# A conditioned block with a long convolution and a gated MLP on one core: block 0 in four real products, two split pieces at the start of stages 1 and 2, and another order of the turns

## The chip, the cores and the metric

The kernel runs on one core of a Trainium2 chip. The metric is the device time of one execution in microseconds (us), the median of several runs. All inputs are bfloat16 and come from HBM.

## The reference

There are 2048 rows x of 576 columns. From a condition vector c comes a modulation of six rows of 576, by one small matrix product. The first half of the block is a layer norm with shift and scale, multiplied by a long causal convolution of a gated sequence; the second half is a layer norm with shift and scale and a SwiGLU MLP with 4608 hidden columns.

```python
mod = (silu(c) @ w_mod).reshape(1, 6, 1, -1)         # sa, ca, ga, sb, cb, gb
h  = layernorm(x) * (1 + ca) + sa
kv = conv4(k, shift_k) * v                           # 4 taps along the rows, per column
y  = causal_conv(kv, ssm_k) + kv * ssm_D             # 2048 taps per column
x  = x + ga * (h * y)
h  = layernorm(x) * (1 + cb) + sb
x  = x + gb * ((silu(h @ w1) * (h @ w3)) @ w2)
```

## The kernel before

**Blocks of the convolution.** The rows are cut into eight blocks of 256. A block's kv rows and a block's filter taps are each taken through a short transform, which is a matrix product on TensorE with cosine and sine matrices (`Fb` for rows, `Fk` for taps). A block has 128 frequencies for even and 128 for odd indices. The spectrum X of kv has six planes of 576 columns: real part, imaginary part and their sum, twice (`x_spectrum`, with the sums added by `x_sums`). The filter's spectrum W has four planes (`w_spectrum`); from the W of two neighbouring blocks DVE makes V, again with six planes (`v_block`). A complex product is so done with three real products, X times V plane by plane (`pair`), and the results of all pairs of blocks that belong to one output block are added in z. `real_parts` and `inverse` bring z back to rows: two matrix products for the even and two for the odd frequencies for each half of the rows. Then ScalarE copies the result out, DVE multiplies it with the gate and adds it to x (`residual`), the second layer norm is taken (`quick_stats` on DVE or `ln_sums` on ScalarE), and the normed rows go to `h2row`.

**Turning rows.** The MLP needs its input with the columns on the partitions. `turn_all` turns 256 rows from `h2row` to `h2T`, for the first two blocks on TensorE and later by two transposing loads on SyncE's queue (L819). `modulate` then applies shift and scale to five tiles, on ScalarE (L834) or, with quick, on DVE (L832). `h2row` is one buffer, `h2T` two.

**The MLP.** It runs over four stages of 512 rows, so one stage takes two blocks, an even and an odd one. A stage has a stream and a down projection. The stream goes over nine pieces of four chunks of 128 hidden columns. For each piece w1 and w3 are loaded into one of three buffers (`load_w13`, L965 and L966); TensorE does the gate and the up product (L1014 and L1025), ScalarE the silu and a copy, and DVE their product (L1039). The buffer `wst[2]` also holds the four slots of w2 in the down projection, where two halves of 288 columns are done one after the other, each in nine w2 pieces (L1123, L1134). A w2 piece is loaded into a slot when the piece four before it is done.

**Order.** Block 0 is written out by hand in `first_block`, with the order of TensorE, ScalarE and DVE fixed. It ends with block 0's turned rows. Then `conv_second` (block 1's convolution) runs beside `stream` on block 0's 256 rows alone, for `N1 = 24` of the 36 chunks. Stage 0 does the odd 256 rows of those chunks (short pieces of 256 rows, whose weights are loaded again, but for the last two) and all 512 rows of the other twelve. Beside each stage r = 0, 1, 2 runs `conv(2r + 2)`, the convolution of the next stage's two blocks. It is a generator whose steps have a cost in us, mostly DVE time; after each piece of MLP work `advance` gives it time at a rate `CONV_US[r] / time`. `end` runs what is left of it.

In stage r's down projection the next stage's odd block ends:

```python
if h == 1 and f0 // W2C == TURN and r + 1 < NRB:
    self.end()
    self.turn_all(2 * r + 3)
    if 2 * r + 5 < NBLK:
        self.pair_taps(2 * r + 5)
    self.modulate(2 * r + 3, r > 0)
```

The even block of the next stage is turned and modulated earlier, within `outcome` of the odd one. Older X and V come back from DRAM on SyncE's queue (`get`), some of them during the down projections. Within an engine the build puts instructions in an order by their dependencies and by estimated times, so that later work can stand ahead of earlier work where nothing forbids it; `behind` and `issue_after` forbid it.

**Taps.** The taps of a block are loaded either as they lie (`load_k`) and turned on TensorE (`k_rows`), which is so for blocks 0 and 1, or by a transposing load (`load_taps`, L303), after which `pair_taps` sorts the rows into pairs with four copies from SBUF to SBUF (L312) into `kT`, a single buffer.

Of the kernel before, what the change touches and what calls it, by code (L numbers as in the profile page):

```python
# [25 lines left out]
FC = 4  # L26
# [3 lines left out]
CONV_US = (72.0, 97.0, 108.0)  # L30
RATE1 = 1.8
FIRST_DUE = 12.0
N1 = 24
# [5 lines left out]
TURN = 7  # L39
# [9 lines left out]
class _Kernel:  # L49
    def __init__(self, ctx, tc, q, k, v, shift_k, ssm_k, ssm_D, w1, w3, w2, c, w_mod, out):  # L50
# [21 lines left out]
        self.last_w2 = None  # L72
# [66 lines left out]
    def early_loads(self):  # L139
# [10 lines left out]
        self.load_mod(0, 3)  # L150
# [154 lines left out]
    def pair_taps(self, s):  # L305

        nc = self.nc
        self.kT = self.kvp.tile([P, 2, D], BF16, name="kT", tag="kT")
        taps = self.knat[:].rearrange("p a b -> p (a b)")
        for half in range(2):  # L310
            for cc in range(2):
                nc.sync.dma_start(self.kT[64 * half:64 * half + 64, cc, :],  # L312
                                  taps[cc:P:2, half * D:(half + 1) * D])
# [347 lines left out]
    def first_block(self):  # L661
# [17 lines left out]
        self.waves(0)  # L679
        self.warm(3, self.h2T[0][:, 0, :])  # L680
        sums = [self.small.tile([P, 1], F32, name="l1" + k, tag="sr" + k) for k in "um"]
        self.run_all(self.k_rows(0))
        self.cond_silu()
        self.warm(4, self.h2T[0][:, 0, :])
# [6 lines left out]
        self.load_k(1)  # L691
        self.run_all(self.w_spectrum(0))
        self.cond()
        self.run_all(rows)
        mean, rstd = self.quick_stats(x1[:, 1, :], "l1")
        nmr = self.small.tile([P, 1], F32, name="l1nm", tag="nmr1")
        nc.gpsimd.tensor_mul(nmr[:], mean, rstd)
        nc.gpsimd.tensor_single_scalar(nmr[:], nmr[:], -1.0, op=ALU.mult)
        self.run_all(self.x_spectrum(0))
        self.run_all(self.v_block(0))  # L700
# [4 lines left out]
        self.load_gb()  # L705
        self.whole_turns(0, True)
        self.waves(0, True)
        X, V = self.X[0], self.V[0]
        self.accs[0] = z = self.acc.tile([P, 6, D], BF16, name="z0", tag="z0")
        for o in (0, 3):  # L710
            nc.vector.tensor_add(X[:, o, :], X[:, o + 1, :], X[:, o + 2, :])
            nc.vector.tensor_mul(z[:, o:o + 3, :], X[:, o:o + 3, :], V[:, o:o + 3, :])
            nc.vector.tensor_add(z[:, o + 1, :], z[:, o, :], z[:, o + 1, :])
            nc.vector.tensor_sub(z[:, o, :], z[:, o, :], z[:, o + 2, :])
        self.mod_piece(2)
        self.ln_sums(x1, 0, sums[0], sums[1], 0)
        scales = [self.ln_shift(*self.ln_var(*sums, "l1", nc.gpsimd), nc.gpsimd), (rstd, nmr)]
# [559 lines left out]
```

## Time and profile before

The median of three runs is 509.51 us (508.95 to 510.03). The profiled execution spans 507.3 us, with a mean granted TensorE clock of 0.997.

| stretch, us from the start | what runs | length | PE busy | DVE busy |
|---|---|---|---|---|
| 0 to 33.7 | block 0 | 33.7 | 29.14 | 27.87 |
| 33.7 to 66 | MLP for block 0's rows, block 1's convolution | 32.3 | 32.22 | 29.33 |
| 66 to 123.5 | stage 0, stream | 57.5 | 55.00 | 52.80 |
| 123.5 to 164.7 | stage 0, down | 41.2 | 38.33 | 36.82 |
| 164.7 to 242.2 | stage 1, stream | 77.5 | 77.50 | 60.71 |
| 242.2 to 281 | stage 1, down | 38.8 | 37.74 | 20.53 |
| 281 to 358.9 | stage 2, stream | 77.9 | 77.78 | 73.71 |
| 358.9 to 396.7 | stage 2, down | 37.8 | 37.01 | 18.43 |
| 396.7 to 467 | stage 3, stream | 70.3 | 70.30 | 13.31 |
| 467 to 507.3 | stage 3, down and the end | 40.3 | 35.52 | 5.82 |

PE is TensorE, PEld its weight loads (which run beside the matmuls), DVE is VectorE, ACT ScalarE, POOL GpSimd, SP SyncE, and SPq the queue on which SyncE issues transfers. A line of the order of time has the start, the time, the engine, the line of the kernel, the operation, the tiles (written from read), the number of instructions, and in brackets how long the engine was idle before it and what ended that. Stage boundaries are taken from TensorE's first matmul of each.

### The profile page before, as it was taken

Reading aid. Unit: us, or ns where it says so; the run is one execution under the profiler, and the core shown is the slowest. Engines: PE = TensorE matmul, PEld = TensorE weight load, DVE = VectorE, ACT = ScalarE, POOL = GpSimd, SP = SyncE. Lnnn points to the kernel's source line nnn. Section 1 sums busy time; section 2 is a strip of 40 time slices with the busy share of each in tenths; the row PEclk is TensorE's granted clock in tenths of the full one; section 3 lists DMA queues with packets and bytes.
Section 4 is the critical chain, followed back from the end, with each engine's and each line's share of the span. In section 5 each row is a group of like instructions: output and inputs, shape, how many; then the busy total and the mean of one; then the engine's idle time right before and its main releaser. Section 6 shows DMA issues by size and latency. Waiting matters only on the chain.

```text
span 507.3 us, 8873 instructions
## 1 busy us (share of the span) xinstructions
PE 490.5 (97%) x3530; PEld 287.9 (57%) x3530; DVE 339.3 (67%) x448; ACT 283.9 (56%) x565; POOL 23.2 (5%) x43
## 2 busy tenths in 40 slices
PE   6999999999998999999999999999999999999996
PEld 2767775547776444343777443434677544444774
DVE  8799899898997586997176999799762321112012
ACT  5758679659343588569450455976824355555000
POOL 4200000000001000000000000000000000000000
PEclk9989999999999999999999999999999999999999
DMA  8987997759999895358799996644575554460562
GB/s 281 329 190 217 293 296 205 203 172 311 269 365 299 281 327 166 111 148 250 202 294 332 309 301 226 209 116 165 154 176 125 170 177 140 143 187 1 140 170 65
DMA packets 115037, 107.99 MB, mean 213 GB/s; under 512 B 20339, under 2 KB 107572, under 8 KB 114996
## 3 DMA queue, kind: packets, MB, share of 16 engines
q1 hardware_dynamic: 114974, 107.41, 71.3%
q8 instruction: 28, 0.46, 0.4%
q14 instruction: 13, 0.11, 0.1%
q10 hardware_dynamic: 22, 0.01, 0.0%
HBM read 92.46 MB, written 9.44 MB: 201 GB/s over the span
## 4 chain that ended last, share of the span: by engine, by line
PE 68%; DVE 12%; DMA 9%; ACT 4%; issue 2%; SPq 1%; POOL 1%; POOLq 0%; DVEq 0%; ACTq 0%
PE ps L1014 29%; PE ps L1078 14%; PE ps L1134 14%; PE ps L1025 4%; DMA V<-Vd 4%; DVE p L438 3%; DMA wst<-in_B_w_dram 2%; PE ps L333 2%; DMA kh<-in_A_k_dram 2%; PE ps L572 2%; PE ps L347 1%; ACT junk L469 1%; DVE og L1159 1%; DVE z L440 1%; DVE z L433 1%
## 5 line engine op out<-in xcount | busy, mean ns | idle before, releaser
L1014 PE MATMUL ps<-h2T,wst 128*128 128x512 bf16 (+1 forms) x1056 | 200.8, 341 | 0.9 <-ACT h2T L834 0.3
L1134 PE MATMUL ps<-wst,h 128*128 128x288 bf16 x1152 | 145.5, 286 | 4.6 <-DMA wst<-in_B_w_dram 3.3
L1014 PEld LDWEIGHTS <-wst 128*128 128x128 bf16 x1056 | 100.2, 98 | 86.8 <-issue 15.3
L1134 PEld LDWEIGHTS <-h 128*128 128x128 bf16 x1152 | 112.5, 98 | 36.3 <-issue 7.2
L1032 ACT ACTIVATE h<-ps 128x512 bf16<-128x512 f32 x108 | 64.8, 600 | 79.8 <-PE ps L1025 51.6
L1078 PE MATMUL ps<-h2T,wst 64*128 64x512 bf16 x648 | 70.3, 376 | 0.0
L1036 ACT CAST u<-ps 128x512 bf16<-128x512 f32 x108 | 63.3, 586 | 0.0
L438 DVE TENSOR_TENSOR p<-X,V 128x3456 bf16<-128x3456 bf16 x28 | 54.7, 1954 | 4.6 <-DMA V<-Vd 4.0
L440 DVE TENSOR_TENSOR z<-z,p 128x3456 bf16<-128x3456 bf16 x28 | 54.6, 1951 | 0.1
L1078 PEld LDWEIGHTS <-wst 64*128 64x128 bf16 x648 | 31.3, 94 | 38.3 <-DVE og L1159 0.2
L1105 DVE TENSOR_TENSOR h<-h,u 128x1024 bf16<-128x1024 bf16 x18 | 12.5, 692 | 58.1 <-ACT u L1102 58.1
L1039 DVE TENSOR_TENSOR h<-h,u 128x1024 bf16<-128x1024 bf16 x54 | 36.9, 685 | 14.1 <-ACT u L1036 14.1
L1099 ACT ACTIVATE h<-ps 128x512 bf16<-128x512 f32 x36 | 21.5, 597 | 39.8 <-PE ps L1078 39.8
L469 ACT ACTIVATE junk<-x 128x576 bf16<-128x576 bf16 x54 | 37.1, 687 | 3.1 <-DVE x L587 2.5
L1159 DVE TENSOR_TENSOR og<-ps,gbrow 128x576 bf16<-128x576 f32 (+1 forms) x18 | 12.3, 687 | 36.8 <-PE ps L1134 36.3
L1025 PE MATMUL ps<-h2T,wst 64*128 64x512 bf16 (+1 forms) x264 | 33.3, 341 | 0.1
L1102 ACT CAST u<-ps 128x512 bf16<-128x512 f32 x36 | 20.9, 580 | 0.0
L1025 PEld LDWEIGHTS <-wst 64*128 64x128 bf16 x264 | 8.5, 94 | 21.5 <-issue 18.9
L834 ACT ACTIVATE h2T<-h2T,sbcol,cbcol 128x256 bf16<-128x256 bf16 x20 | 10.4, 590 | 18.2 <-DMA h2T<-h2row 18.2
L599 ACT ACTIVATE h2row<-x,l2n,l2r 128x576 bf16<-128x576 bf16 (+1 forms) x24 | 13.8, 654 | 9.2 <-DVE l2n L487 9.2
L367 DVE TENSOR_TENSOR kv<-kv,p 128x1152 bf16<-128x1152 bf16 x24 | 18.1, 753 | 0.3
L361 DVE TENSOR_TENSOR p<-kh,shk 128x3456 bf16<-128x3456 bf16 x8 | 15.6, 1953 | 0.6 <-ACT shk L210 0.6
(142 smaller groups left out, 366.2 us busy)
## 6 DMA issues: line engine op xcount, KB each, us to landing
wst<-in_B_w_dram SPq DMA_DIRECT2D x80, 512.0 KB, 5.0
wst<-in_B_w_dram SPq DMA_DIRECT2D x72, 288.0 KB, 3.9
wst<-in_B_w_dram SPq DMA_DIRECT2D x80, 64.0 KB, 3.2
kh<-in_A_k_dram SPq DMA_DIRECT2D x7, 720.0 KB, 6.6
X<-Xd SPq DMA_DIRECT2D x5, 864.0 KB, 5.9
V<-Vd SPq DMA_DIRECT2D x5, 864.0 KB, 6.0
Xd<-X SPq DMA_DIRECT2D x4, 864.0 KB, 7.9
Vd<-V SPq DMA_DIRECT2D x4, 864.0 KB, 5.2
```

What stands on the lines that cost most here:

```text
L438: nc.vector.tensor_mul(p[:], X[:], V[:])
L440: nc.vector.tensor_add(z[:], z[:], p[:])
L469: self.nc.scalar.activation(junk[:], src[:, i, :], func, scale=scale, accum_out=out[:, col:col + 1])
L1014: nc.tensor.matmul(gus[k][:, i, a * n:(a + 1) * n], w[:, 5 * i + ct, (fi + a) * P:(fi + a + 1) * P], hT[:, ct, t0:t1], start=(first and ct ...
L1025: nc.tensor.matmul(gus[k][:, i, a * n:(a + 1) * n], w[rows, 4, (fi + a) * P:(fi + a + 1) * P], hT[rows, 4, t0:t1], start=(first and a == 0 ...
L1032: nc.scalar.activation(self.h3[:, f:f + m, t0:t1], gus[k][:, 0, :].rearrange("p (a t) -> p a t", a=m), ACT.Silu)
L1036: nc.scalar.copy(self.u[:, k % 2, :], gus[k][:, 1, :])
L1039: nc.vector.tensor_mul(h3, h3, self.u[:].rearrange("p b (a t) -> p (b a) t", a=m))
L1078: nc.tensor.matmul(gus[k][:, i, :], ws[fc][rows, 5 * i + ct if ct < 4 else 4, cols], hT[rows, ct, :], start=swap == 0 and ct == 4, stop=sw ...
L1099: nc.scalar.activation(h3, gus[k][:, 0, :], ACT.Silu)
L1102: nc.scalar.copy(self.u[:, k % 2, :], gus.pop(k)[:, 1, :])
L1134: nc.tensor.matmul(acc[t], self.h3[:, f0 + f, t * P:(t + 1) * P], w[:, f, :], start=(f0 + f == 0), stop=(f0 + f == NF - 1))
```

## The change

It has four parts. Block 0 no longer makes V and its three-product form; it multiplies X with W in four real products a parity, and TensorE adds them in the inverse product, which so has eight terms instead of four for each half of the rows, one of them with a negated cosine matrix (`minus`). What block 1 needs of V, X's sums and its own filter spectrum goes to `conv_second`; block 1's taps come by a transposing load. Statistics of both halves of block 0's rows are taken early on DVE, mod piece 2 is done ahead of `x_spectrum`, and w_mod's first three pieces come in three loads. Second, `N1` is 28: seven pieces, not six, run beside block 1. Third, in stages 1 and 2 the first two pieces run for the even 256 rows and then for the odd ones, so that the odd rows may come later: the convolution beside the stage before goes on into the stream, and the next one begins after the even pieces. Fourth, the turns of the even blocks wait (`pending`) for a set place in the down projection, and `pair_taps` uses two copies instead of four and stands at the last w2 piece. For the last stage the odd rows are still turned within the down projection, at piece 8 instead of 7.

```diff
-CONV_US = (72.0, 97.0, 108.0)
+CONV_US = (72.0, 104.0, 118.0)
-N1 = 24
+N1 = 28
-TURN = 7
+EVEN, MOD, TURN = 4, 6, 8
+SOLO = 2
+QUICK1 = True
@@ early_loads
-        self.load_mod(0, 3)
+        for m in (2, 1, 0):
+            self.load_mod(m, 1)
@@ pair_taps
-            for cc in range(2):
-                nc.sync.dma_start(self.kT[64 * half:64 * half + 64, cc, :],
-                                  taps[cc:P:2, half * D:(half + 1) * D])
+            nc.sync.dma_start(self.kT[64 * half:64 * half + 64], taps[:, half * D:(half + 1) * D])
@@ first_block
+        minus = self.kvp.tile([P, P], BF16, name="minus", tag="Wo")
+        nc.gpsimd.tensor_single_scalar(minus[:], self.Fb[:, 0, 0], -1.0, op=ALU.mult)
+        self.cond_silu()
         self.warm(3, self.h2T[0][:, 0, :])
         self.run_all(self.k_rows(0))
-        self.cond_silu()
-        self.warm(4, self.h2T[0][:, 0, :])
+        self.cond()
+        self.warm(3, self.h2T[0][:, 0, :])
...
-        self.load_k(1)
+        self.load_taps(1)
         self.run_all(self.w_spectrum(0))
-        self.cond()
         self.run_all(rows)
-        mean, rstd = self.quick_stats(x1[:, 1, :], "l1")
...
-        self.run_all(self.x_spectrum(0))
-        self.run_all(self.v_block(0))
...
+        self.pair_taps(1)
+        scales = [self.quick_stats(x1[:, cc, :], "l1") for cc in range(2)]
+        self.mod_piece(2)
+        self.run_all(self.x_spectrum(0))
         self.whole_turns(0, True)
+        z = [self.acc.tile([P, 6, D], BF16, name=f"z{i}", tag=f"z{i}") for i in range(2)]
+        for e in range(2):
+            Xe = X[:, 3 * e + 1:3 * e + 3, :]
+            nc.vector.tensor_mul(z[e][:, 0:2, :], Xe, W[:, 2 * e:2 * e + 2, :])
+            nc.vector.tensor_mul(z[e][:, 2:4, :], Xe, _ap(W, (2 * e + 1) * D, [[-D, 2], [1, D]]))
...
+            nc.scalar.activation(hg[:, cc, :], x1[:, cc, :], ACT.Identity, bias=nmr[cc][:, 0:1], scale=scales[cc][1])
         self.waves(0, True)
-        for o in (0, 3):
-            nc.vector.tensor_add(X[:, o, :], X[:, o + 1, :], X[:, o + 2, :])
-            nc.vector.tensor_mul(z[:, o:o + 3, :], X[:, o:o + 3, :], V[:, o:o + 3, :])
-            nc.vector.tensor_add(z[:, o + 1, :], z[:, o, :], z[:, o + 1, :])
-            nc.vector.tensor_sub(z[:, o, :], z[:, o, :], z[:, o + 2, :])
...
-        ps = [self.inverse(0, cc) for cc in range(2)]
+        ps = [whole(cc) for cc in range(2)]
         self.run_all(self.gate(0))
-        self.run_all(self.k_rows(1))
         self.mod_columns()
-        self.run_all(self.w_spectrum(1))
@@ outcome
+                self.turn_pending()
                 for cc in range(2):
                     self.normed_act(s, cc, *scales)
+                if s % 2 == 0:
+                    self.pending = s
@@ conv_second
         yield from self.kv_rows(1)
+        yield from self.w_spectrum(1)
+        yield from self.v_block(0)
+        yield from self.x_sums(0)
         yield from self.v_block(1)
@@ stream
+            if r > 0 and k == SOLO * FC // 2:
+                self.end()
+                with self.tc.issue_after(self.end_w2):
+                    self.turn_all(2 * r + 1)
+                self.modulate(2 * r + 1, QUICK1)
+                self.begin(self.conv(2 * r + 2))
@@ down
+                if h == 1 and f0 // W2C == EVEN and r + 1 < NRB:
+                    self.turn_pending()
+                if h == 1 and f0 // W2C == MOD and r + 1 < NRB:
+                    self.modulate(self.raw, QUICK)
                 if h == 1 and f0 // W2C == TURN and r + 1 < NRB:
-                    self.end()
-                    self.turn_all(2 * r + 3)
-                    if 2 * r + 5 < NBLK:
+                    if r + 2 == NRB:
+                        self.end()
+                        with self.behind(nc.sync):
+                            self.turn_all(2 * r + 3)
+                        self.modulate(2 * r + 3, True)
+                    else:
                         self.pair_taps(2 * r + 5)
-                    self.modulate(2 * r + 3, r > 0)
@@ row_blocks
-                self.begin(self.conv(s0), FIRST_DUE if r == 0 else 0.0)
+                if r == 0:
+                    self.begin(self.conv(s0), FIRST_DUE)
...
-                new = [(n1 + i, 0, RB, b, None) for i, b in enumerate((2, 1, 2))]
-                again = [(fc, 256, 512, b, None) for fc, b in enumerate((0, 0, 1, 0))]
+                new = [(n1 + i, 0, RB, b, None) for i, b in enumerate((2, 0))]
+                again = [(fc, 256, 512, b, None) for fc, b in enumerate((1, 2, 1, 0, 1))]
...
+                if r + 1 < NRB:
+                    first = [(j[0], t0, t0 + B, j[3] if t0 == 0 else None, j[4] if t0 == 0 else None)
+                             for t0 in (0, B) for j in jobs[0:SOLO]]
+                    jobs[0:SOLO] = first
             self.down(r, rate)
-            self.end()
```

## The prediction, made before the changed kernel was run

> **What bounds the kernel now.** I read the page's busy shares first, then the busy time by stage, then the order of time around each place where TensorE stands still.
>
> ```profile
> PE 490.5 (97%) x3530; PEld 287.9 (57%) x3530; DVE 339.3 (67%) x448; ACT 283.9 (56%) x565; POOL 23.2 (5%) x43
> PEclk9989999999999999999999999999999999999999
> ```
>
> TensorE is the bound nearly everywhere. A saving must take work off it, start it earlier, or close one of its gaps. The busy time by stage (stage, its length, then busy time of PE, PEld, DVE, ACT, POOL, clock, DMA share, GB/s) says where gaps are:
>
> ```profile
> 0.00:33.70 33.70, 29.14 (x214) 18.34 (x215) 27.87 (x62) 21.22 (x42) 10.55 (x28) 0.95 1.01 294
> 33.70:66.00 32.30, 32.22 (x302) 25.41 (x301) 29.33 (x43) 23.85 (x48) 1.79 (x3) 1.00 0.78 241
> 66.00:123.50 57.50, 55.00 (x394) 32.70 (x393) 52.80 (x64) 43.80 (x92) 1.90 (x2) 1.00 0.76 223
> 123.50:164.70 41.20, 38.33 (x308) 29.73 (x306) 36.82 (x43) 18.25 (x37) 2.96 (x2) 1.00 1.12 314
> 242.20:281.00 38.80, 37.74 (x305) 29.71 (x304) 20.53 (x27) 12.40 (x25) 0.69 (x1) 1.00 0.94 285
> 358.90:396.70 37.80, 37.01 (x300) 28.85 (x299) 18.43 (x32) 16.37 (x36) 1.38 (x2) 1.00 0.66 170
> ```
>
> Rows 4 to 6 are the down projections of stages 0, 1 and 2. The same matmuls stand in each, yet stage 0 takes 41.2 us. From start to start a 288-column matmul takes 0.1225 us, so 288 of them take 35.3. Stage 0 has 16 more of the convolution (2.0) and one early matmul (0.2): 37.5, so 3.7 are lost. Stage 1 has the same 16: 38.8 - 37.3 = 1.5 lost. Stage 2 has 8: 37.8 - 36.3 = 1.5 lost. In stage 0's stream, six short pieces (256 rows, 4.14 us each: 32 matmuls in 3.60 and 8 in 0.54) and three full ones (8.2) make 49.4, 34 convolution matmuls 4.2; of 57.5 about 3.9 are lost. The order of time shows stage 0's large gap and its neighbours on the queue:
>
> ```profile
> 145.89 4.53 SPq L1123 DMA_DIRECT2D wst<-in_B_w_dram  x3
> 150.48 1.66 SPq L312 DMA_DIRECT2D kT<-knat  x2
> 152.30 0.47 SPq L1123 DMA_DIRECT2D wst<-in_B_w_dram  x1
> 152.81 1.29 SPq L312 DMA_DIRECT2D kT<-knat  x2
> 154.20 8.00 PE L1134 MATMUL ps<-wst,h 128*128 128x288 bf16 x64 [1.93 <-DMA wst<-in_B_w_dram]
> 155.85 2.57 SPq L819 DMA_TRANSPOSE h2T<-h2row  x2
> 161.80 2.57 ACT L834 ACTIVATE h2T<-h2T,sbcol,cbcol 128x256 bf16<-128x256 bf16 x5 [4.95 <-DMA h2T<-h2row]
> ```
>
> A w2 load was issued at 152.30, behind two kT copies on SyncE's queue, and TensorE waited 1.93 us for it. The odd rows of the next stage were modulated at 161.80 to 164.37, just when TensorE needed them. The page puts 4% of the ending chain on V reloads, which share the queue and engines with w2. In block 0 the chain runs through DVE and TensorE together:
>
> ```profile
> 23.36 3.85 PE L267 MATMUL ps<-crep,h 128*128 128x1 bf16 x60
> 25.89 0.76 DVE L579 TENSOR_TENSOR hg<-ps,hg 128x576 bf16<-128x576 f32 x1
> 27.14 3.49 PE L333 MATMUL ps<-kT,Fk 128*128 128x288 bf16 x16
> 30.47 1.46 PE L659 MATMUL ps<-shk,ident 128*128 128x512 bf16 x6
> 31.76 0.44 PE L611 MATMUL ps<-ident,h2row 128*128 128x128 bf16 x5
> ```
>
> The first residual row waits until 25.89, and the first turn until 31.76. The first MLP matmul is at 33.75.
>
> **What the Trainium skill says.** "TensorE: Matmul & The Clock Gate", Part 1 (the HAM clock gate): the array runs at 1.2 or 2.4 GHz by its recent activity, in free-running windows of about 3.4 us. The trace agrees: the granted clock was 0.5 from 26.53 to 29.94, after the 60 one-column matmuls, and the 288-column ones of L333 then lie 0.240 us apart instead of 0.1225. The same page, "Architectural detail": ACT and DVE are strict FIFO, and TensorE only pulls weight loads ahead; so a matmul whose operand is late holds all behind it, as at 154.20. "DMA: Bandwidth & Descriptors", "Issuing engines are not separate DMA queues": all transfers end on the same 16 engines. Stage 0's down, with a DMA share of 1.12 and 314 GB/s, has no room to spare. "VectorE: DVE Perf Modes", the perf-mode tier table: tensor_scalar on bf16 in SBUF has a faster mode than tensor_tensor. The trace has it: five modulations take 1.37 us on DVE (L832) and 2.57 on ACT (L834).
>
> **The change part by part.**
>
> 1. Block 0. DVE loses V (0.46 + 0.76 + 0.75) and eight operations (4.9 us); it gains four products of 1152 elements at about 0.67, two tiny ones, and a second set of statistics (1.2). The statistics stand before the spectra, beside TensorE's filter spectrum. With mod piece 2 moved ahead of x_spectrum, X is copied to SBUF by about 18.9 rather than 17.6. Then come products to 20.7, arow and brow to 22.2, gate to 23.65, and the first residual row at 23.65 instead of 25.89: 2.2 us earlier. TensorE's side: `whole` needs 32 matmuls for 16 (+2.0), the next filter's 10 transposes (0.56) and 16 matmuls (3.4 at the low clock) go. I place `whole` at 20.55 to 24.6, L267 to 28.45, six warm-up matmuls to 29.75, the first turn there: 2.0 earlier if the clock is full, 0.7 if the half clock falls on the warm-ups (1.3 more). ACT's inverse waves come after hg, at about 21.6 to 22.6, hidden by `whole` for the even rows. w_mod in three loads of 1152-byte rows: 576 packets at 59 ns (such packets at 12 to 34 us) over 16 engines are 2.1 us each, so piece 2 lands by about 10, before its use at 14.3. I take -1.6; bounds -0.3 to -2.4.
> 2. The next filter's spectrum moves into block 1: 16 matmuls at 0.1225 on a busy TensorE, +1.95. Its taps come by a transposing load (4.6 us to landing for the natural ones before) and pair copies, more than 10 us ahead of use. The two pair copies wait on SyncE's queue for the transpose; behind them are the next taps and w13 loads, which wait for a free buffer anyway.
> 3. V of block 0 (2.0) and its sum (0.75) move to DVE beside block 1: +2.75, and one more hide product of 0.69. Block 1 grows by a short piece (4.14), so TensorE has some 6 us more there than DVE needs; cost 0 on the path.
> 4. Pieces: twelve short and three full (74.3) become fourteen short and two full (74.4). Stages 1 and 2 split two pieces each: 4 x 4.14 - 2 x 8.2 = 0.16 a stage. Sum +0.4.
> 5. Turn order in stages 0 and 1. The odd rows' turn and modulation leave the down's end; kT copies are two, not four, and stand last on the queue. The even turn stands behind the fifth w2 load of the second half. That is a new wait: queued behind its two issues (2.57 us) is the next w2 load, for TensorE. But that load waits about 2 us for its buffer anyway. Of 3.7 lost in stage 0 I keep 0.8 (-2.9), of stage 1's 1.5 I keep 0.55 (-0.95), since V reloads still share the queue.
> 6. The new wait at the odd pieces. Before, the odd residual (L587) ended at 145.7 and the rows were ready at 164.4. DVE starts 1.6 earlier with 3.4 more to do, and modulates 1.2 faster: ready at about 165. TensorE begins stage 1 at 164.7 - 1.6 + 1.95 + 0.1 - 2.9 - 0.55 = 161.7 and the odd pieces 8.3 later, at 170. Five us of slack: 0. The next convolution is begun 8.3 later too, but DVE was busy for only 56.7 of 83 us in stage 1 (173 to 256): hidden. In stage 2 it was busy for 81.4 of 94, so this holds less well there.
> 7. Stage 2's end: the w2 load before the odd turn instead of behind it; 1.5 becomes 1.0 (-0.5).
> 8. Losses of block 1 and the stream of stage 0 (0.7 + 3.9, such as 0.61 for ACT at 72.38 and 0.64 for DVE at 107.77): -0.55, since block 1's turned rows come in time.
>
> Sum: -1.6 + 1.95 + 0.4 - 2.9 - 0.95 - 0.5 - 0.55 = -4.15, so 505.4 us.
>
> **The rivals.**
>
> A. All gaps close: -2.4 in block 0, -3.5, -1.5, -1.2 in the three downs, -2.05 elsewhere, +2.35 of work: -8.3, 501.2 us. For it: every gap has a waiting record. Against it: DVE is still over 90% busy in stage 0.
>
> B. The w2 waits stay, because the reloads still take DMA engines that are full there: -1.6 + 2.35 - 1.2 = -0.45, 509.1 us. For it: the DMA share of 1.12. Against it: the kT copies stood directly ahead of the late load.
>
> C. Slower. The half clock falls on the first MLP matmuls (-0.3 in block 0, +1.2 after). Short pieces outrun their two weight buffers: in block 1 a load was issued at 38.09, its last part at 39.72 landed 4.9 later, at 44.6, and a piece lasts 4.14; convolution matmuls filled that time so far; three waits of 0.8. The odd rows are late by 2. In all -0.3 + 1.2 + 2.35 + 2.4 + 2.0 - 4.35 = +3.3, 512.8 us.
>
> **How the numbers follow.** The forecast has 0.55, A 0.15, B 0.17, C 0.13. About half of B lies within 0.2% (1.0 us) of before, so faster 0.75, same 0.10, slower 0.15. The range takes A, B and half the way to C: 501.0 to 511.0.
>
> **What would show it.** Right: the first L1014-like matmul at about 32; stage 0's down without a wait for w2 over 0.5; the odd pieces without a wait for h2T. Wrong: the first MLP matmul after 33, a wait of TensorE for wst in a short piece, or an odd piece waiting for DVE's modulation.

## The result, and the profile after

The changed kernel takes 516.01 us (median of 6 runs, 512.94 to 518.01), the kernel before, run beside it, 509.28 us (508.56 to 510.33). The ratio is 1.0127, with a 95% interval of 1.0089 to 1.0165. So it is slower, by 6.7 us, where 505.4 us was forecast. The profiled execution spans 515.7 us against 507.3.

The page's busy shares and granted clock of the changed kernel, in 40 equal slices:

```profile
PE 494.4 (96%) x3720; PEld 312.3 (61%) x3735; DVE 340.6 (66%) x456; ACT 279.3 (54%) x555; POOL 24.0 (5%) x38
PEclk9989998999899999999999999999999999999999
```

DVE's work is 1.3 us more than before. The clock now dips twice more after block 0, in the slices that begin at 77 and 129 us. The busy time by stage of the changed kernel, in the columns of the table shown before (block 0; beside block 1; stage 0's stream; its down; then the downs of stages 1 and 2):

```profile
0.00:32.95 32.95, 28.40 (x201) 17.90 (x203) 25.12 (x60) 16.30 (x32) 9.16 (x23) 0.95 0.99 295
32.95:74.02 41.07, 39.47 (x358) 29.99 (x357) 32.51 (x50) 28.70 (x58) 1.79 (x3) 1.00 0.82 210
74.02:134.84 60.82, 53.47 (x393) 34.12 (x393) 54.52 (x68) 42.70 (x89) 3.47 (x3) 0.94 0.78 235
134.84:173.20 38.36, 37.98 (x307) 29.72 (x305) 34.27 (x36) 14.69 (x29) 2.27 (x1) 1.00 1.03 293
...
250.96:290.60 39.64, 38.03 (x306) 29.75 (x305) 24.64 (x33) 15.17 (x30) 2.75 (x2) 1.00 1.00 267
...
368.15:405.20 37.05, 36.79 (x301) 29.15 (x298) 21.87 (x33) 17.63 (x37) 1.79 (x2) 1.00 0.67 169
```

Block 1's stretch grew by 8.6 us (from 32.4) and stage 0's stream by 3.3 (from 57.5). Stage 0's down lost 2.9 and the rest changed little. In block 1 TensorE stands for only 1.6 us (before, for 0.1), but DVE has 32.5 us of work in 41.1, so it is idle for 8.6 us; before it was idle for 3.0. In the stream both have holes: TensorE 7.3 us, DVE 6.3.

The order of time of block 0 after the change, for TensorE and DVE:

```profile
23.84 0.76 DVE L580 TENSOR_TENSOR hg<-ps,hg 128x576 bf16<-128x576 f32 x1
24.90 3.92 PE L270 MATMUL ps<-crep,h 128*128 128x1 bf16 x60
...
29.57 1.91 PE L660 MATMUL ps<-shk,ident 128*128 128x512 bf16 x4 [0.22 <-issue]
...
31.27 0.49 PE L612 MATMUL ps<-ident,h2row 128*128 128x128 bf16 x5
```

The first residual row starts at 23.84, 2.05 us earlier than before. Then the half clock (27.95 to 31.36) lies on the six warm-up matmuls of L660, which take 0.43 us each (four of them from 29.57 to 31.27), and the first turn waits behind them on TensorE until 31.27, only 0.5 earlier than before. The first MLP matmul is at 33.30, not 33.75.

The largest hole of TensorE is in stage 0's stream. SyncE's queue and the matmul that waited, in the order of time of the changed kernel:

```profile
66.80 0.53 SPq L287 DMA_DIRECT2D kh<-in_A_k_dram  x1
67.46 0.35 SPq L293 DMA_DIRECT2D vt<-in_A_v_dram  x1
67.85 0.92 SPq L318 DMA_DIRECT2D x<-in_A_q_dram  x2
...
69.29 0.33 SPq L446 DMA_DIRECT2D Xd<-X  x1
...
69.73 1.57 SPq L314 DMA_DIRECT2D kT<-knat  x2
...
73.56 1.96 DVE L362 TENSOR_TENSOR p<-kh,shk 128x3456 bf16<-128x3456 bf16 x1 [2.02 <-DMA kh<-in_A_k_dram]
...
81.50 0.90 PE L348 MATMUL ps<-kT,Fk 128*128 128x288 bf16 x6 [3.41 <-DMA kT<-knat]
```

The chain of waits for this window has the copies' second half as one transfer (start, length, what):

```profile
70.61 10.75 DMA kT<-knat
...
81.50 0.90 PE ps L348 x6
```

The copies went out behind all of block 2's loads and the spill of X, landed 11.1 us after their issue, and TensorE stood for 3.41 us. DVE, too, stood for 2.02 us until block 2's `kh` came. After TensorE's hole the clock was halved from 82.56 to 85.97.

This is one of five stops of TensorE (times in which it stands still between two matmuls) in the stream. The last three stand closer to its end:

```profile
117.65 0.41 PE L348 MATMUL ps<-kv,Fb 128*128 128x288 bf16 x2 [1.13 <-ACT u L1057]
...
127.86 0.61 PE L1035 MATMUL ps<-h2T,wst 128*128 128x256 bf16 x4 [0.79 <-ACT junk L470]
129.66 2.12 PE L1035 MATMUL ps<-h2T,wst 128*128 128x256 bf16 x12 [1.19 <-DMA wst<-in_B_w_dram]
```

The clock was halved again from 130.35 to 133.76.

### The profile page after: what moved, and what is told of

Same layout as the page of the kernel before. It is cut to its first block, busy times and chain, and to the rows that moved or that the text cites. A ratio compares the mean times of both kernels' runs of the same rounds, so it can differ in the third digit from the quotient of the medians.

```text
span 515.7 us, 9268 instructions
## 1 busy us (share of the span) xinstructions
PE 494.4 (96%) x3720; PEld 312.3 (61%) x3735; DVE 340.6 (66%) x456; ACT 279.3 (54%) x555; POOL 24.0 (5%) x38
## 4 chain that ended last, share of the span: by engine, by line
PE 83%; DMA 10%; ACT 2%; SPq 2%; issue 1%; DVE 1%; POOL 0%; DVEq 0%; POOLq 0%; ACTq 0%
PE ps L1035 33%; PE ps L1163 23%; PE ps L1105 14%; DMA wst<-in_B_w_dram 7%; PE ps L1046 5%; PE ps L348 2%; DMA kT<-knat 2%; PE ps L573 2%; PE ps L334 1%; DMA knat<-in_A_ssm_k_dram 1%; PE ps L241 1%; PE ps L733 1%; PE ps L660 1%; PE ps L270 1%; DVE og L1193 1%
## 5 line engine op out<-in xcount | busy, mean ns | idle before, releaser
L1035 PE MATMUL ps<-h2T,wst 128*128 128x256 bf16 (+1 forms) x1202 | 202.5, 320 | 4.0 <-DMA wst<-in_B_w_dram 2.1
L1035 PEld LDWEIGHTS <-wst 128*128 128x128 bf16 x1216 | 116.8, 99 | 77.2 <-issue 11.9
L1105 PEld LDWEIGHTS <-wst 64*128 64x128 bf16 x648 | 36.1, 94 | 34.1 <-PE ps L1163 0.7
L441 DVE TENSOR_TENSOR z<-z,p 128x3456 bf16<-128x3456 bf16 x28 | 54.6, 1951 | 0.2
L470 ACT ACTIVATE junk<-x 128x576 bf16<-128x576 bf16 x52 | 35.8, 689 | 4.4 <-DVE x L588 4.0
L1046 PE MATMUL ps<-h2T,wst 64*128 64x256 bf16 (+1 forms) x304 | 33.4, 322 | 0.1
L1046 PEld LDWEIGHTS <-wst 64*128 64x128 bf16 x304 | 10.6, 95 | 19.4 <-issue 16.5
L434 DVE TENSOR_TENSOR z<-X,V 128x3456 bf16<-128x3456 bf16 x7 | 13.7, 1955 | 13.1 <-DMA V<-Vd 9.8
L350 ACT CAST W<-ps 128x576 bf16<-128x576 f32 x12 | 7.6, 649 | 22.3 <-PE ps L348 22.3
```

Of the source, the lines that this page charges most:

```text
L441: nc.vector.tensor_add(z[:], z[:], p[:])
L470: self.nc.scalar.activation(junk[:], src[:, i, :], func, scale=scale, accum_out=out[:, col:col + 1])
L1035: nc.tensor.matmul(gus[k][:, i, a * n:(a + 1) * n], w[:, 5 * i + ct, (fi + a) * P:(fi + a + 1) * P], hT[:, ct, t0:t1], start=(first and ct ...
L1046: nc.tensor.matmul(gus[k][:, i, a * n:(a + 1) * n], w[rows, 4, (fi + a) * P:(fi + a + 1) * P], hT[rows, 4, t0:t1], start=(first and a == 0 ...
L1105: nc.tensor.matmul(gus[k][:, i, :], ws[fc][rows, 5 * i + ct if ct < 4 else 4, cols], hT[rows, ct, :], start=swap == 0 and ct == 4, stop=sw ...
```

## The experiments

Each ratio is against the kernel before, run on the same chip beside it. In an expectation a letter stands for the theory that it, or the first expectation with that letter, names; in the last four, Q is SyncE's order and D a stretch chained through several engines.

The table gives lengths in us from the traces, and DVE's work and idle time from block 1's start to stage 1's. The boundaries stand up to 0.4 us ahead of the first matmul's record. Each row is one execution, while a ratio is that of the medians of all. The traced execution lay 4.4 us above its kernel's median in e7, 2.9 in e10, 2.5 in e3, 1.7 in the changed kernel, and 2.4 below it in e4. Block 0 is the same code in before, e1, e5, e10, e11 and e14 and took 33.4 to 34.2. So a microsecond or two between two rows of one column says little.

```
kernel                  block 0  block 1  s0 stream  s0 down  sum of the 3  DVE busy  DVE idle   ratio
before                    33.4     32.4      57.5      41.2       131.2      119.1     12.1      1
after                     33.0     41.1      60.8      38.3       140.2      121.3     18.9      1.0127
e1  turns only            33.4     32.4      57.5      41.0       130.9      118.4     12.5      0.9984
e2  after, N1 24          34.0     38.1      59.5      40.4       138.1      121.3     16.9      1.0133
e3  loads earlier         34.8     49.2      54.7      39.8       143.7      120.9     22.7      1.0212
e4  four copies           33.6     41.6      56.2      39.5       137.3      121.1     16.2      1.0155
e5  before, N1 28         34.2     37.9      56.4      41.5       135.8      119.4     16.5      1.0132
e6  two warm-ups          31.9     43.6      55.6      39.8       139.1      120.9     18.2      1.0126
e7  late spill            34.3     41.4      61.4      39.8       142.7      121.2     21.4      1.0120
e8  filter in block 0     37.3     39.9      59.4      38.9       138.2      120.7     17.5      1.0173
e9  V in the holes        33.6     40.5      58.3      40.0       138.8      119.4     19.4      1.0194
e10 before, 28, kh early  33.8     38.1      56.7      42.2       137.1      119.2     17.9      1.0108
e11 turns, slower pace    33.7     32.4      58.9      41.5       132.9      112.5     20.4      1.0284
e12 after, GpSimd copies  33.5     41.0      60.0      41.8       142.9      120.9     22.0      1.0224
e13 e9, GpSimd copies     34.4     42.1      58.9      41.9       142.9      120.1     22.8      1.0222
e14 e1, GpSimd copies     34.1     32.4      60.5      41.3       134.2      119.4     14.8      1.0063
e15 e9, late taps         34.2     40.3      58.3      39.8       138.4      119.2     19.3      1.0134
```

Length is busy plus idle, so the table alone names no cause. But it says that DVE's work is much the same in all but e11, which puts some off to stage 1, and that what differs is how long DVE stands.

**e1_turns_only: parts three and four alone.** Block 0, what follows it in block 1, and `N1 = 24` are as before; the split pieces, the turn order, two kT copies and the rates are the change's.

```diff
-CONV_US = (72.0, 97.0, 108.0)
-TURN = 7
+CONV_US = (72.0, 104.0, 118.0)
+EVEN, MOD, TURN = 4, 6, 8
+SOLO = 2
```

> The kernel before with only the later parts of the change: split pieces in stages 1 and 2, the new turn order, two kT copies, the new rates. Block 0, conv_second and N1 = 24 are those of before. Theory 1 (the loss comes from the crowded transfers and short pieces around the end of block 1 and in stage 0's stream): faster than before by about 3.5 us, near 505.5, with stage 0's down near 38.3 us instead of 41.3. Theory 2 (the split and the turn order themselves cost): slower than before, 511 or more. If the late parts only shift the wait: within 1 us of 509.3.

Measured: 509.54 us against 510.76, ratio 0.9984 (0.9959 to 1.0009). Stage 0's down stays at 41.0 us. Two of TensorE's waits in e1's list of waits (us in total, times, longest):

```profile
PE ps L1150 <- DMA wst<-in_B_w_dram: 2.4, 4, 1.3
PE ps L1150 <- DVE h L1047: 2.0, 2, 1.1
```

The waits for w2 fell from 3.3 us over all stages to 2.4, in stage 0's down from 1.9 to 0.8. But in stage 0's down there is more of a wait for DVE's product of gate and up, 2.0 instead of 0.6. So the turn order shortens the wait that it aims at, and TensorE stands as long for the next thing.

**e2_n24: the change without the seventh piece.**

```diff
-N1 = 28
+N1 = 24
-new = [(n1 + i, 0, RB, b, None) for i, b in enumerate((2, 0))]
-again = [(fc, 256, 512, b, None) for fc, b in enumerate((1, 2, 1, 0, 1))]
+new = [(n1 + i, 0, RB, b, None) for i, b in enumerate((2, 1, 2))]
+again = [(fc, 256, 512, b, None) for fc, b in enumerate((0, 0, 1, 0))]
```

> The changed kernel with N1 = 24 and the buffer order of before, so six pieces beside block 1. Theory 1a (the seventh short piece and the fifth reload cost): most of the loss goes, 508 to 510 us, no wait of TensorE for kT over 1 us. Theory 1b (block 0's work moved into block 1 costs): it stays at 514 or more, since block 1's DVE work no longer fits beside six pieces and TensorE waits for its turned rows by some 3 us.

Measured: ratio 1.0133 (1.0091 to 1.0176). Of TensorE's list of waits in e2:

```profile
PE ps L605 <- DVE l2mv L499: 1.3, 1, 1.3
...
PE ps L1035 <- ACT h2T L635: 1.0, 3, 0.7
PE ps L605 <- DVE h2row L505: 0.8, 1, 0.8
```

With six pieces TensorE has nothing left before block 1's rows are turned (L605). So the seventh piece covers a real hole, but block 0's new form and what it moves already cost as much as the whole change. In the stream, once the rows are turned, no stop of e2 is longer than 0.65 us; the stops of the changed kernel are not there.

**e5_before_28: the seventh piece alone.** The kernel before with `N1 = 28` and its buffers, nothing else.

> The kernel before with N1 = 28 and the buffer order that goes with it, nothing else. Theory T (the seventh short piece crowds transfers and loads at the end of block 1 and in stage 0): 2 to 5 us slower than before, with waits of TensorE for kT or wst around 70 us. Theory W (the loss is the DVE and TensorE work moved into block 1): within 1.5 us of before.

Measured: 516.80 us, ratio 1.0132 (1.0078 to 1.0187). This one edit also costs as much as the whole change. Block 1 grows by 5.5 us, and stage 0's stream, which has 4.0 us less of pieces (one more short piece, one full piece less), shrinks by 1.2. It has five stops, 6.0 us in sum, much like those of the changed kernel. The first is 0.75 us for kT; the last three are

```profile
112.73 0.41 PE L347 MATMUL ps<-kv,Fb 128*128 128x288 bf16 x2 [1.12 <-ACT u L1036]
...
123.44 0.61 PE L1014 MATMUL ps<-h2T,wst 128*128 128x256 bf16 x4 [1.29 <-ACT X L349]
124.86 1.48 PE L1014 MATMUL ps<-h2T,wst 128*128 128x256 bf16 x12 [0.81 <-DMA wst<-in_B_w_dram]
```

The second and longest, in e5's order of time:

```profile
86.96 1.96 DVE L433 TENSOR_TENSOR z<-X,V 128x3456 bf16<-128x3456 bf16 x1
87.01 2.47 POOL L481 TENSOR_TENSOR l1r<-l1v,neghalf 128x2 f32<-128x2 f32 x1 [23.90 <-DVE l1v L477]
...
89.52 0.16 DVE L487 TENSOR_TENSOR l1n<-l1s,l1r 128x2 f32<-128x2 f32 x1 [0.59 <-POOL l1r L481]
...
89.71 1.62 ACT L533 ACTIVATE hg<-x,l1n,l1r 128x576 bf16<-128x576 bf16 x2 [1.52 <-DVE l1n L487]
91.24 0.56 ACT L1036 CAST u<-ps 128x512 bf16<-128x512 f32 x1
...
91.86 0.41 PE L347 MATMUL ps<-kv,Fb 128*128 128x288 bf16 x2 [2.07 <-ACT u L1036]
```

GpSimd's tiny power began just behind a DVE product and took 2.47 us, not its usual 0.69. ScalarE waited 1.52 us for what follows from it, with the MLP's copy queued behind, and TensorE stood for 2.07 us until that copy freed its buffer in PSUM, the memory that takes TensorE's results. Before, the same product came after the power, which took 1.20 us beside a shorter one; ScalarE waited 0.84 us there and TensorE not at all.

**e3_early_loads, e4_four_copies, e7_late_spill: relieving the kT wait.** The changed kernel with block 2's loads one piece earlier; with four kT copies as before; and with the spill of X in the stream instead of ahead of the copies.

```diff
e3: self.block_two if fc == n1 - 1 -> n1 - 2
e4: pair_taps of the kernel before
e7: keep_x(0) moved from block_two to the load of the first full piece of stage 0
```

> The changed kernel with block_two (loads of kv 2, x 2, x 3 and the spill of X 0) at the sixth of the seven pieces instead of the seventh. Theory 1c (these transfers stand right ahead of the kT copies and delay them): the 3.4 us wait for kT and DVE's 2.0 us wait for kh go, and with them the half clock at 82 us: 4 to 6 us faster than the changed kernel, 510 to 512. If kT is late for the kT copies' own shape, the wait stays and the time is near 516.

> The changed kernel with four kT copies as before instead of two. If the two-copy form is slower to land, the wait for kT falls from 3.4 us to under 1 and the time to 512 or less. If the queue of transfers ahead is the cause, the wait stays or grows by 1 us (two more issues at 0.6 each), and the time is within 2 us of the changed kernel's 516.

> The changed kernel with the spill of X 0 (864 KB) in the first full piece of stage 0 instead of right ahead of the kT copies. Theory T: kT lands 2 to 3 us earlier, TensorE's wait of 3.4 us falls under 1.5 and the half clock at 82 us goes: 3 to 5 us faster than the changed kernel. If the queue's other loads set it: within 1.5 us of 516.

Measured: 1.0212 (1.0161 to 1.0264), 1.0155 (1.0104 to 1.0207) and 1.0120 (1.0064 to 1.0176). The kT wait fell from 3.4 us to under 0.3, 1.4 and under 0.3, and no time was won that these runs can tell. In e3 TensorE stood 4.7 us for the seventh piece's weights behind the early loads. In e4 the waits for ScalarE's copy in the convolution came to 2.9 us and those for stream weights to 3.4, in e7 to 2.8 and 6.0; in the changed kernel they are 1.8 and 2.1.

**e6_two_warmups: the half clock of block 0.** The changed kernel with `self.warm(2, busy)` for `self.warm(6, busy)`.

> The changed kernel with two warm-up matmuls instead of six ahead of the first turn. If block 0 ends late because the warm-ups run at the half clock (0.427 us each), the first turn comes 1.6 us earlier, near 29.7, and the first MLP matmul near 32: 1 to 1.7 us faster than the changed kernel. If the six are needed to bring the clock back, the half clock reaches into the MLP and the time stays or grows by up to 1.7 us.

Measured: ratio 1.0126 (1.0071 to 1.0181), 515.74 us. Block 0 ended 1.0 us earlier and block 1 took 2.5 us longer. So in these two traces the microsecond saved in block 0 was not kept, and the times can't be told from the changed kernel's.

**e8_filter_in_block0 and e9_v_in_holes: each half of what was moved into block 1.** Both are e2's kernel. In e8 block 1's filter spectrum is made in block 0 again, from taps loaded as they lie, and V and X's sums stay in block 1. In e9 it is the other way round.

```diff
e8 first_block: +self.load_k(1) ... +self.run_all(self.k_rows(1)) ... +self.run_all(self.w_spectrum(1))
e8 conv_second: -yield from self.w_spectrum(1)
e9 first_block: +self.run_all(self.v_block(0)) ... +self.run_all(self.x_sums(0))
e9 conv_second: -yield from self.v_block(0)
e9 conv_second: -yield from self.x_sums(0)
```

> The changed kernel with N1 = 24 and block 1's filter spectrum (natural load, ten transposes, sixteen matmuls) back in block 0, where it stood before; V and the X sums of block 0 stay in block 1. If the moved TensorE work and the taps' way cost: block 1 loses 2 us or more of its 38.1 (N1 = 24, all moved), and the time is near 512. If DVE's 2.75 us and the wait for the turned rows set block 1: it stays near 38 and the time at 515 or more.

> The changed kernel with N1 = 24, and with V of block 0 and the sums of X 0 back in block 0, but placed where DVE stood idle there: V at 14.3 to 18.05 (waiting for X), the sums at 30.2 to 31.9 (waiting for the turn). Block 1's filter spectrum stays in block 1. Theory D (DVE's 2.75 us in block 1 delay the turned rows and TensorE waits for them): block 0 as long as in the changed kernel, block 1 falls from 38.1 (N1 = 24, all moved) to 34.5 us, and the time to 510 to 512. If it is TensorE's moved filter or the taps' transfers: block 1 stays above 37 and the time at 515 or more.

Measured: 1.0173 (1.0109 to 1.0236) and 1.0194 (1.0159 to 1.0228). Undoing either half gains nothing. In e8 block 0 took 37.3 us, 3.3 more than in e2, so part of its cost lies there. The times of DVE's first product with block 1's V and of block 1's last normed row, each from block 1's start, show how late block 1 runs:

```
                        before   e5    after    e2     e8     e9
first product with V(1)   8.7    8.8    14.2   14.0   11.8   13.6
last normed row ends     29.6   29.6    36.1   38.1   39.8   38.7
```

Block 1's convolution is a chain: its filter spectrum, V, the products, the inverse, the residual, the norm, the turn. The spectrum on TensorE and ScalarE, and V of block 0 on DVE, both stand ahead of V of block 1, beside each other: so the later of them counts, not their sum: 11.8 with V alone ahead, 13.6 with the filter alone, 14.0 with both. In the order of time of before, the changed kernel and e8, one after the other:

```profile
42.13 1.95 DVE L433 TENSOR_TENSOR z<-X,V 128x3456 bf16<-128x3456 bf16 x1
...
43.60 0.76 DVE L420 TENSOR_TENSOR V<-W 128x1152 bf16<-128x1152 bf16 x1 [0.95 <-ACT W L337]
47.13 1.95 DVE L434 TENSOR_TENSOR z<-X,V 128x3456 bf16<-128x3456 bf16 x1
...
55.62 0.76 DVE L384 TENSOR_TENSOR X<-X 128x1152 bf16<-128x1152 bf16 x1 [4.43 <-ACT X L337]
```

The chain's end moves by as much as its start and more, so the start is not the whole cause. TensorE also stood 3.0 us for weights in e8 and 2.9 in e9. In e8 it stood 2.02 us for them at 49.02, where the MLP pieces followed each other without convolution matmuls between them, and DVE then stood 4.43 us for the spectrum of block 1's rows; by the last row the delay had grown from 3.1 to 10.2. In e9 the weights came late by SyncE's queue. Its order of time:

```profile
43.29 1.23 SPq L314 DMA_DIRECT2D kT<-knat  x2
43.67 0.76 DVE L420 TENSOR_TENSOR V<-W 128x1152 bf16<-128x1152 bf16 x1 [1.45 <-ACT W L337]
...
47.21 1.30 SPq L306 DMA_TRANSPOSE knat<-in_A_ssm_k_dram  x1
...
48.57 0.57 SPq L986 DMA_DIRECT2D wst<-in_B_w_dram  x1
...
54.11 0.61 PE L1035 MATMUL ps<-h2T,wst 128*128 128x256 bf16 x4 [1.56 <-DMA wst<-in_B_w_dram]
```

DVE waited 1.45 us for the last plane of the filter's spectrum. The next taps' copies waited for the same spectrum to free `kT`, the transposing load for the copies, and the weights stood behind both.

**e10_28_kh_early.** e5 with `load_kv(2)` one piece earlier, since one more piece had put block 2's `kh` from 56.4 to 64.5 us on SyncE's queue.

> The kernel before with N1 = 28 and the load of kh and v for block 2 one piece earlier (the sixth of seven); x and the spill stay at the seventh. In the run with N1 = 28 alone DVE stood idle around 64 to 70 us and began block 2's kv rows at 70.4, when kh landed. Theory K (the late begin of the next convolution is what makes the shorter stream of stage 0 wait): DVE begins near 65, stage 0's stream falls from 56.4 us towards 53.5, and the time by 2 to 3 us, to 513.5 to 515. If the waits come from the order of instructions and from weights: within 1.5 us of 516.8.

Measured: 514.46 us, ratio 1.0108 (1.0070 to 1.0145), not to be told from e5. DVE's idle time in block 1 fell from 4.7 to 3.0 us, and in stage 0's stream it rose from 6.5 to 8.0.

**e11_turns_slow_pace.** e1 with `CONV_US[0]` 64 instead of 72, so that the convolution is spread later.

> The turn-order kernel (block 0, conv_second and N1 of before) with the cost rate of stage 0 at 64 instead of 72, so that less convolution stands ahead of the MLP's own work on DVE. In the turn-order run TensorE waited 2.0 us at the start of the down projection for DVE's h product, which stood behind convolution products. If that order is the cause: these waits fall under 0.7 us and the time to about 508. If DVE is simply full until then, the wait moves and the time stays within 1 us of the turn-order run.

Measured: 523.81 us, ratio 1.0284 (1.0250 to 1.0318). DVE's work left over at stage 1's start made the odd rows late; in e11's order of time:

```profile
183.39 1.37 DVE L841 TENSOR_SCALAR h2T<-h2T,cbcol,sbcol 128x256 bf16<-128x256 bf16 x5 [1.73 <-DMA h2T<-h2row]
...
183.84 2.38 PE L1022 MATMUL ps<-h2T,wst 128*128 128x256 bf16 x10 [4.98 <-DVE h2T L841]
```

TensorE stood for 4.98 us, the half clock followed from 184.2, and stage 1's stream took 88.4 us instead of 77.8. The split pieces give the odd rows some slack, and a rate lower by a ninth uses it up.

**e12, e13, e14: kT copies on GpSimd's queue.** The changed kernel, e9 and e1, with one word changed in `pair_taps`:

```diff
-            nc.sync.dma_start(self.kT[64 * half:64 * half + 64], taps[:, half * D:(half + 1) * D])
+            nc.gpsimd.dma_start(self.kT[64 * half:64 * half + 64], taps[:, half * D:(half + 1) * D])
```

> The changed kernel with the two kT copies of every block issued by GpSimd instead of SyncE, so that they no longer stand behind the block-2 loads and the X spill on SyncE's queue, and no weight load stands behind them. Theory Q (SyncE's order is what holds TensorE): the 3.4 us wait for kT at 77.8 falls under 0.7 us and the stream of stage 0 with it, from 60.8 to about 57.5; the time is 511.5 to 513.5 us, ratio about 1.005. Theory D (the stretch from block 1 to stage 0's stream is chained through DVE, ScalarE and the DMA engines together, so closing one wait opens another): the kT wait shrinks, but stage 0's stream stays above 59.5 or block 1 grows by as much, and the time is 514.5 to 518 us, ratio 1.011 to 1.018.

> e9's kernel (six pieces beside block 1; V and X's sums of block 0 made in block 0) with the kT copies issued by GpSimd. In e9 the w13 loads of the fourth and fifth piece were issued at 48.57 to 53.74, behind two kT copies and a transposing load that waited for the filter spectrum's matmuls, and TensorE stood 1.84 and 1.60 us at 52.3 and 54.5. Theory Q: both stops go, block 1 takes 36.5 to 37.5 us instead of 40.5, time 513 to 516 us. Theory D: block 1 stays above 39 us or stage 0's stream grows, time 517 to 521 us.

> e1's kernel (block 0 and the six pieces as before, with the split pieces and the turn order of the change) with the kT copies issued by GpSimd. Theory Q: the copies stood ahead of weight loads there too, so 506.5 to 508.5 us, ratio 0.993 to 0.997. Theory D: nothing that can be told from e1, 508.5 to 511 us, ratio 0.996 to 1.001.

Measured: 1.0224 (1.0198 to 1.0251), 1.0222 (1.0190 to 1.0254) and 1.0063 (1.0045 to 1.0082), all slower than either theory gave. In TensorE's list of waits in e12

```profile
PE ps L1163 <- DMA wst<-in_B_w_dram: 6.1, 5, 2.7
PE ps L348 <- ACT u L1057: 2.9, 1, 2.9
PE ps L1035 <- DMA wst<-in_B_w_dram: 2.3, 2, 1.2
...
PE ps L1035 <- ACT junk L470: 2.0, 1, 2.0
...
PE ps L348 <- DMA kT<-knat: 0.9, 1, 0.9
```

the kT wait fell to 0.9 us. In its place came a wait of 2.9 us like that of e5 at 91.86 (ScalarE stood 2.40 us for the same statistics), one of 2.0, and 6.1 us for w2 over all stages. In e14, where the copies had cost 0.8 us, TensorE now waited 3.8 us for kT, and e14 was 0.8% slower than e1. So issuing the copies on GpSimd has a price of its own. These runs don't support SyncE's order as the one cause, but they don't test it alone either; e15 comes closer.

**e15_v_in_holes_late_taps.** In e13 the transposing load still stood ahead of the weights, so this run moves that load in e9:

```diff
-        with self.behind(self.nc.sync):
-            self.load_taps(3)
-        yield from self.outcome(1, self.mix(self.filter_ahead(2)), (5.0, 3.5, 0.0, 2.0), quick=True)
+        def ahead():
+            yield -4.0
+            with self.behind(self.nc.sync):
+                self.load_taps(3)
+            yield from self.w_spectrum(2)
+        yield from self.outcome(1, self.mix(ahead()), (5.0, 3.5, 0.0, 2.0), quick=True)
```

> e9's kernel with the transposing load of block 3's taps issued later, in front of block 2's filter spectrum instead of right after the pair copies of block 2. In e13 this load still stood ahead of four weight loads on SyncE's queue: it waited until 48.30 for the copies, and the weights were issued from 49.69 on. Theory Q (SyncE's order): the weights of the fourth and fifth piece go out some 4 us earlier, the stops of TensorE at 52 to 56 us (3.4 in sum) go, block 1 takes 37 instead of 40.5 us and the time is 513.5 to 517 us. Theory D (chained stretch): the stops go, but what DVE has left lengthens the end of block 1 or stage 0's stream, and the time stays at 517.5 to 521 us.

Measured: 517.03 us, ratio 1.0134 (1.0104 to 1.0163), between the two ranges; e9 had 1.0194. In block 1 it is theory D: the stops for weights are gone, and TensorE waits instead for DVE's z,

```profile
PE ps L573 <- DVE z L553: 2.7, 1, 2.7
PE ps L1038 <- ACT X L350: 1.5, 2, 1.3
```

the clock falls from 59.8 on, and block 1 takes 40.3 us instead of 40.5. The gain over e9 that the traces show, 1.4 us, lies in stage 1's down, 39.8 instead of 41.4.

No version beat the kernel before by more than its uncertainty; e1 came nearest.

## Why the prediction was wrong

**Two steps failed: part 3 and part 4, and part 8 with them.** Part 3 said "Block 1 grows by a short piece (4.14), so TensorE has some 6 us more there than DVE needs; cost 0 on the path". Part 4 moved a piece from stage 0's stream into block 1 at +0.1 in sum. Part 8 let the losses of both stretches shrink by 0.55. In the changed kernel block 1 took 41.1 us where the forecast had 38.5 (32.4 + 1.95 + 4.14), and the stream 60.8 where it had 53.0 (57.5 - 4.0 of pieces - 0.5 of losses). The sums of work were near the truth; what they left out is the order within a stretch.

- **Part 3: the work was put ahead of a chain.** With the work moved and six pieces as before (e2), block 1 grew by 5.7 us, where parts 2 and 3 gave 1.95, and the stream by 2.0. e2, e8 and e9 show 3.1 to 5.3 us of delay at the chain's start and 8.5 to 10.2 at the last row. Part 2 priced the filter's spectrum as TensorE work, +1.95, and not as something that block 1's V waits for. The free engine time was there (DVE was idle for 8.6 us of block 1), and did not help.
- **Part 4: the moved piece adds its time to block 1, but does not leave stage 0's stream.** With the piece alone (e5), block 1 grew by 5.5 us against 4.14, and the stream lost 1.2 against 4.0. e5 has five stops in the stream like those of the changed kernel, and e2, without the piece, has none over 0.65 us there after the turn: so these stops come with the piece. In the changed kernel they make 7.2 us, and two windows at half clock can cost up to half of their 6.8. The forecast's 53.0 us was also less than the 54.5 us of work that DVE turned out to have in that stretch (52.8 before). The prediction itself noted against its rival A that "DVE is still over 90% busy in stage 0". Block 2's loads also go out 8 us later (e5), so that DVE begins block 2 later; letting them out earlier (e3, e10) did not help either.
- **The two costs do not add up.** e2 and e5 each cost 1.3%, and so does the change. By the traces block 1 grows by 5.7 and 5.5 us alone and by 8.6 with both, so some 2.6 of the chain's delay and the extra piece lie beside each other. The stream is worse with both (+3.3) than the two alone would make it (+2.0 and -1.2), and stage 0's down is shorter.

**Part 1** was right in its mechanism: the first residual row was forecast at 23.65 and came at 23.84. Of its two cases for the warm-ups the worse came: -0.45 instead of -1.6, in its bounds. In e6, where block 0 was 1.0 us shorter, the time was the same.

**Part 5.** Stage 0's down did shorten by 2.9, as forecast, and the wait for w2 that the forecast aimed at fell from 1.93 us to two of 0.17 and 0.20. But the turn order alone does not give this: in e1 the down stays at 41.0, because waits for DVE's product appear, which the forecast did not have. In the changed kernel they are absent, after a stream that was 3.3 us longer. That the late stream let DVE catch up is likely, and no run separates it; so the right number was in part luck. Stage 1's down grew by 0.8 instead of losing 0.95: its waits for w2 came to 1.5 us instead of 0.9.

**Parts 6 and 7**, and the split pieces of part 4, held: stage 1's stream took 77.8 us against 77.5, its odd pieces did not wait for their rows in the changed kernel (e11 shows what it looks like when they do), and stage 2's down lost 0.7 us against 0.5. The 1.37 and 2.57 us of a modulation, on which part 6 rests, compare DVE with ScalarE; they don't show the faster mode of tensor_scalar against tensor_tensor for which the prediction gives them. Other lines of the trace of before do: from 64 to 576 elements a tensor_scalar (L504) went from 0.29 to 0.43 us, and from 1152 to 3456 a tensor_tensor from 0.75 to 1.95, which is 0.27 against 0.52 ns an element.

**Rival C** had the direction and one of its mechanisms, short pieces that outrun their weights: a wait of 0.92 us for the seventh piece's weights at 69.85 and one of 1.19 in a short piece at 129.66, 2.1 us against its 2.4. These waits, and the first MLP matmul at 33.30, are also two of the prediction's own signs of being wrong. The half clock on the first MLP matmuls and the late odd rows did not come. Its sum of 512.8 was too low, because it had neither the chain nor the stops of ScalarE and kT in the stream.

**What stays open.** Removing a stop in this stretch gave its time back elsewhere in e3, e4, e6, e7, e10, e12 and, in block 1, e15. The replacing waits are named above, but no run gives a rule for which one comes next. So which moves cost the time is shown (e2 and e5), and the waits through which they cost it are seen, but no run gave the time back by removing them. e8 and e9 each undo one half of what was moved out of block 0; no run keeps block 0's four products and undoes both. So what the four products cost or gain by themselves stays open. Moving the power of the statistics off GpSimd was not tried.

## What to carry to other kernels

Before moving work into a stretch with free engine time, ask what in that stretch waits for it: work ahead of the first link of a chain can delay the whole chain even where the engine's sum leaves room. Before taking a piece out of a stage, check that the second busiest engine's work still fits into what is left; here 54.5 us of it stood against 53.0. And test the parts apart: here two parts each cost as much as the whole, and undoing one of them gained nothing.

## What the hardware showed that was not expected

- **GpSimd beside DVE.** In the traces of before, the changed kernel, e2, e5 and e12 a power of 128x2 took 0.69 or 0.70 us when DVE had no product running, 1.07 to 1.21 when it began just after one of 1152 elements had begun, 1.67 to 1.68 when a second product followed at once, and 2.27 to 2.47 after one of 3456. Each of these ended 0.5 to 0.6 us after the last such product; in e5 the product ended at 88.92, and the power 0.56 us later. The Trainium skill, "SBUF — State Buffer", section "Who interferes with whom", says that a DVE tensor_tensor with both inputs in SBUF contends with GpSimd's reads, and that the one that comes later blocks. The trace agrees.
- **Half clock without a whole idle window.** The Trainium skill, "TensorE: Matmul & The Clock Gate", Part 1 (the HAM clock gate), has the clock fall after an idle window of about 3.4 us. In the changed kernel the window before 130.35 had 1.44 us of busy time in 3.41, and the one before 82.56 had 1.06, and both were followed by half clock. So at 130.35 stops of 0.8 and 1.2 us close together were enough, while in e5 a single stop of 2.07 us at 91.86 was not followed by it. The three starts of half clock in the changed kernel, 27.95, 82.56 and 130.35, lie 54.6 and 47.8 us apart, which is 16 and 14 times the 3.41 us that each lasted; this agrees with the page's free-running windows.
- **A small copy behind large loads.** The kT copies within SBUF landed 3.1 to 11.1 us after their issue in the changed kernel, 5.2 in the median; the longest, at 69.73, came right behind block 2's loads and a spill.
